# Turning q of two more batches by DMA, with a new written order, in a fused attention and channel-mix kernel

## The chip, the cores and the metric

The kernel runs on one core of a Trainium2 chip. The metric is the device time of one execution in microseconds (us); three timed executions and one profiled execution of the kernel before are known.

## The reference

There are 8 batches, 8 heads, 576 positions and 64 elements to a head. Attention here is linear: `q` is softmaxed over the head's elements, `k` over the positions, and the two are joined by a 64 x 64 matrix for each head. The result is the input of a channel mix over 512 channels with a hidden size of 1024.

```python
q_s = softmax(q, axis=-1); k_s = softmax(k, axis=2)
kv  = einsum('bhsd,bhse->bhde', k_s, v)
x   = einsum('bhsd,bhde->bhse', q_s, kv)          # heads side by side: (8, 576, 512)
x_prev = x moved down by one position, a zero row first
xk = mu_k * x + (1 - mu_k) * x_prev;  xr = mu_r * x + (1 - mu_r) * x_prev
k  = maximum(xk @ w_k, 0)                         # 512 -> 1024
out = sigmoid(xr @ w_r) * ((k * k) @ w_v)         # 1024 -> 512
```

## The kernel before

**Attention.** A batch `b` is worked in two groups `g` of four heads. A load brings q, k or v of a group in float32 into one of 11 `raw` buffers (L212, issued on GpSimd's queue for batches 1 to 7). For each group: ScalarE takes the exponentials of q and k (`expq`, `expk`, L345) and casts v (`cast`, L352); VectorE sums the exponentials of q over the head (`rsum`, L360), takes the reciprocal (`rrec`, L364) and scales (`scale`, L369), which gives q in `qs`, positions on the partitions. The next product needs q with the head's elements on the partitions, so q has to be turned. There are three ways in the code:

- Batches 0 and 1 (`FUSED`): TensorE turns q by products with an identity (`T` steps, L386), ScalarE and VectorE copy the result from PSUM (`qt`, L395). Here mu is folded into the 64 x 64 matrix, so that `X` steps (L520) give xk and xr at once and the `x` steps copy them out (L530 to L535). In names such as X1001 the digits are batch, group, which of xk (0) and xr (1), and half of the positions.
- Batches 2 to 4: the turning products stand inside the block of the group that is named `TKV` or `B` (L386), ScalarE copies q out (`qt`, L397).
- Batches 5 to 7 (`CROSS`): SyncE issues one DMA that turns all of `qs` into `qt` (`tq`, L559). It waits for `scale` and has no work on TensorE or ScalarE.

```python
        crossed = b in CROSS
            def block():
                if turn_x: turn_x[0](qtp)        # x of the group before
                if not crossed: transpose_q(qtp)
                kv(qtp)
        if crossed:
            qcopy = add("SP", lambda: kn.nc.sync.dma_start_transpose(
                out=turned_sb(), in_=kn.qss[qs.index][:].rearrange("p j c -> p (j c)")),
                scaled, [qt], [qs], name=f"tq{tag}")
        else:
            qcopy = add("ACT", lambda: copy_qt(qtp), [tr, wdone], [qt], [qtp], name=f"qt{tag}")
```

A block of batch 2 or later does three things on TensorE: x of the group before (L576), the turn of its own q (where it is not crossed), and kv (L419). `rz` and `w` (L426, L436) make the 64 x 64 matrix of a group from kv. `xb` and `xs` (ScalarE, L581 and L584) copy x out, and VectorE mixes it with the row before: `edge` (L589), `diff` (L593), four `sc` (L598), two `mix` (L603). `mix` with third digit 0 gives xk, with 1 xr.

**Channel mix.** It runs over two rings of 2304 columns (four batches). `k<unit>_<n>` steps are products of xk with one 128-wide piece of w_k over the 256 to 512 columns of a unit (L680), `relu` is on ScalarE (L659), `sq` on VectorE (L669). Tiles of 128 rows follow: `r` (xr with w_r, L713), `th` (tanh on ScalarE, L718), `v<tile>_<part>` (k squared with w_v, L733), `o` (VectorE, L739) and two stores on SyncE's queue (`st`, L749). A `.2` after a k step of units 0 to 2 is the half of its product that needs group 1.

**Order.** Nothing is scheduled at run time beyond semaphores: `ORDER` is one long written list of steps. Each engine and each DMA queue takes its own steps in the order in which they stand in it; the number behind a colon is the buffer, an engine ahead of `!` puts the step on that engine. So a step that waits holds up all that stands behind it on the same engine. (`!` has effect on loads, `cast`, `wp` and `x` steps; `qt` and `rest` have their engine written in their own code.)

**Filling.** The `fill` and `fillgap` steps (L302, L311) are products of zeros of 512 and 256 columns, of which no one reads the result. They stand in the first 15 us of TensorE's list.

Of the kernel before, what the change touches and what calls it, by code (L numbers as in the profile page):

```python
# [67 lines left out]
v3_1 DVE!qt100:1 expk101 qt101 X1101:1 KV10 edge10 ACT!x1101 edge11 rz10:0 v0_2 kvn10:1 v3_2
POOL!wp100:1 o0 v1_2 load21v0:4 X1001:1 expq200:0 o1 X1000:0 X1110:3 load21k0:5 x1001 st1 v2_0:0
x1000 load30k0:7 DVE!x1110 cast200:2 X1111:1 load31q0:6 rsum200:1 X1100:0 k2_1:2 load40q0:8 x1100  # L70
v2_1 k2_7:3 expq210:2 wp101 rrec200 o3 k2_1.2 v2_2 load61v0:9 relu2_1:0 k2_2:1 o2 k2_7.2 expq300:1
load50k0:10 k2_0:2 x1111 k2_2.2 relu2_7:1 sq2_1 k2_5:0 rsum300:0 load31k0:0 k2_0.2 expk200:1
k2_4:3 X1010:0 relu2_2:2 X1011:1 scale200:1 load40v0:1 k2_4.2 relu2_0:0 k2_3:1 x1010 k2_6:2 sq2_7
cast210:0 k2_3.2 sq2_0 load30v0:2 k2_5.2 x1011 k2_6.2 relu2_5:1 rsum210:2 TKV20:0 relu2_4:0
load40k0:3 expk210:2 r5:0 rz20:1 rrec300 rrec210 r7:3 w20:0 th5:4 sq2_5 load31v0:4 scale210:2
relu2_3:1 r6:0 qt20:0 r4:1 load41q0:5 scale300:0 th7:5 B21:1.0 expq310:0 sq2_2 sq2_4 r8:3 rz21:2
relu2_6:2 sq2_3 load41v0:6 rsum310:3 xs20:0 th4:6 v4_0:2 xb20 v6_0:1 sq2_6 w21:1 th6:7 rrec310
edge20 v4_1 diff20:0 qt21:2 v6_1 scale310:1 th8:8 X21:0.1 v5_0:0 xb21:1 sc2001:0 sc2000 v4_2 o6
xs21 expk300:0 v7_0:3 edge21 st6 mix200 v5_1 st0 cast300:1 diff21:1 load51q0:7 st3 v7_1 sc2101:1
st2.2 expk400:1 sc2100 load60q0:2 mix210 st0.2 TKV30:0 cast310:2 o7 st3.2 load41k0:3 k3_4:1 st2 o5  # L80
expq400:2 k3_0:3 load70v0:4 sc2011:2 rz30:0 sc2111:0 k3_6:0 w30:2 relu3_4:0 sc2110 load70q0:8
sc2010 relu3_0:1 o4 k3_1:1 expk310:2 mix201 k3_5:3 mix211 relu3_1:2 load61q0:0 k3_3:2 qt30:1 sq3_1
sq3_4 k3_2:1 sq3_0 relu3_3:2 rsum400:1 relu3_5:0 B31:1.0 relu3_2:1 rrec400 k3_7:2 sq3_3 xb30:0
sq3_2 sq3_5 v8_0:3 xs30 relu3_6:2 rz31:1 scale400:2 r9:1 relu3_7:1 expq410:1 v10_0:0 sq3_7 w31:0
# [6 lines left out]
load50v0:1 sq4_6 k5_5 relu4_0:1 mix311 k5_2:1 relu5_4:0 k5_7 sq4_0 cast410:2 k4_2:3 sq5_4 w40:1
scale510:1 k4_5:2 relu4_2:1 load71k0:6 relu5_6:0 k4_1:3 mix301 expq600:2 sq4_3 k5_3 sq4_2 k4_4:0
relu4_1:2 sq5_6 load60k0:2 rsum500:3 relu4_5:1 k5_0:3 relu4_4:0 r14:2 qt40:2 rsum600:1 k5_1 r13:0
th14:7 sq4_1 cast500:0 rrec600 B41:1.0 rrec500 sq4_5 sq4_4 th13:4 load60v0:1 scale600:2 v13_0:2
xs40:1 relu5_0:2 r15:0 xb40 rz41:0 sq5_0 w41:2 v12_0:3 relu5_2:1 edge40 diff40:1 th15:8 v15_0:1
qt41:1 scale500:0 v13_1 expk510:1 sc4001:0 tq50:0 B50:0.1 o13 st10.2 cast600:2 v12_1 rsum700:2
v15_1 xb41:0 rz50:1 o12 r16:0 expk610:2 w50:0 st12 sq5_2 v14_0:2 sc4010:1 st13.2 sc4000 xs41 o15
expk710:0 st13 v16_0:3 edge41 st12.2 mix400 th16:9 r17:1 st7.2 sc4011 expq710:2 diff41:0 tq51:2
B51:1.0 sc4110:2 cast610:0 v16_1 rrec700 sc4101:0 sc4100 v17_0:0 mix410 expk600:1 rz51:2 o16 v14_1
th17:1 mix401 expq610:1 k6_4:3 o14 k6_0:1 v17_1 sc4111 xs50:1 st14 xb50 w51:1 mix411 st4.2 k6_1  # L100
k6_2:2 rsum610:0 st1.2 relu6_0:0 B60:1.0 st11.2 k6_3 tq60:1 xb51:0 sq6_0 k6_5 st15.2 rz60:0
rrec610 edge50 r19:1 o17 st11 relu6_4:2 diff50:1 xs51 st16 k6_6:0 th19:4 r18:3 edge51 diff51:0
expk700:1 k6_7 sc5101:0 r20:1 sc5000:1 th18:3 sc5100 relu6_2:1 sq6_4 r21:3 w60:2 relu6_6:0 sq6_2
sq6_6 v19_0:2 th21:5 sc5010:2 mix510 th20:6 v18_0:0 sc5001 mix500 v19_1 sc5011 B61:0.1 o19 k7_3:3
sc5110:0 mix501 k7_2:1 scale700:0 relu7_3:2 xb60:1 k7_0:2 scale610:1 relu7_2:1 k7_6:3 relu7_0:0
k7_1:1 sc5111 tq61:0 rz61:1 sq7_3 tq70:2 mix511 v18_1 relu7_6:2 st14.2 cast700:1 sq7_6 k7_4:2
sq7_2 rsum710:1 relu7_1:2 k7_5:3 relu7_4:1 r23:1 o18 sq7_1 k7_7:2 sq7_0 th23:0 w61:0 relu7_5:2
r25:0 xs60 relu7_7:0 edge60 sq7_4 B70:1.0 sq7_7 rrec710 v21_0:1 diff60:1 xs61:0 xb61 v22_0:3
sc6000:1 th25:2 edge61 diff61:0 v20_0:2 cast710:2 sc6001 r22:0 rz70:2 sc6110:2 sq7_5 w70:1 v21_1
mix600 th22:7 sc6100:0 B71:0.1 sc6101 mix610 v22_1 o21 k8_1:0 scale710:2 k8_3:1 relu8_1:1 o22  # L110
tq71:1 v20_1 st19 sc6111 mix611 k8_0:0 st22 st15 sc6011:1 v23_0:3 rz71:0 relu8_0:0 st19.2 xb70:0
sq8_0 k8_4:0 st16.2 st18.2 xs70 v23_1 relu8_3:2 relu8_4:0 sq8_3 k8_5:1 sq8_4 edge70 k8_2:0 w71:2
relu8_5:2 diff70:0 sc6010 X71:1.0 o20 k8_6:1 mix601 st20.2 k8_7:2 relu8_6:0 st18 sq8_5 sq8_1 r26:1
st20 sc7010:0 relu8_7:2 sc7001:2 st17 relu8_2:1 sc7000 r28:2 xs71:1 sq8_2 xb71 o23 r24:0 th28:8
# [784 lines left out]
```

## Time and profile before

| | us |
|---|---|
| three runs | 198.82, 198.87, 199.62 (median 198.87) |
| the profiled execution | 198.85 |
| its span, first to last instruction | 196.9 |
| busy in the span: TensorE, VectorE, ScalarE | 188.0, 151.9, 134.9 |

A row of the profile's timeline gives start, duration, engine, line of the kernel, operation, what it writes and reads, shapes and count; a bracket at its end tells how long the engine had been idle and what released it. PE is TensorE, DVE VectorE, ACT ScalarE, POOL GpSimd, SP SyncE. In the views of windows a row is a stretch of the span with the busy time of each engine, the clock that TensorE was granted (PEclk, 1.00 is full), the mean busy share of the 16 DMA engines and what they moved.

### The profile page before, as it was taken

The page shows a single profiled execution, that of the slowest core. Times are in us where ns is not written, and L with a number is a line of the kernel's source. Part 1 is how long each engine was busy: PE and PEld are TensorE (multiplying, and loading weights), DVE is VectorE, ACT ScalarE, POOL GpSimd, SP SyncE. Part 2 cuts the span into 40 slices and gives each one's busy share as a digit, 9 for nine tenths or more (in the row PEclk, how much of TensorE's full clock was granted, in tenths as well). Part 3 has the DMA queues.
Part 4 walks back from the last instruction along what each step waited for, and adds up shares of the span by engine and source line. Part 5 has one row for each costly group of instructions (what it writes and reads, how often), then busy time and mean ns, then how long its engine had stood idle before and what let it go on. Part 6 is the DMA issues. An engine that isn't in the chain of part 4 may idle for free.

```text
span 196.9 us, 4779 instructions
## 1 busy us (share of the span) xinstructions
PE 188.0 (95%) x1894; PEld 96.1 (49%) x1916; DVE 151.9 (77%) x343; ACT 134.9 (69%) x213; POOL 47.7 (24%) x79
## 2 busy tenths in 40 slices
PE   7799989899999999999999999999999999999992
PEld 2268654445454455455544564444444444444441
DVE  1957599789999999999999998989868553534421
ACT  3755759879999999989999984676166345433311
POOL 5849576098312503333200000000000000000000
PEclk9966999999999999999999999999999999999998
DMA  6999999979999998989878582060274011065835
GB/s 188 348 203 295 348 256 359 398 239 392 392 389 387 315 416 297 298 312 413 318 148 168 103 171 64 16 134 0 57 168 107 0 42 41 19 142 118 202 83 160
DMA packets 23702, 41.87 MB, mean 213 GB/s; under 512 B 9460, under 2 KB 12800, under 8 KB 23680
## 3 DMA queue, kind: packets, MB, share of 16 engines
q0 software_dynamic: 9504, 28.00, 44.0%
q1 hardware_dynamic: 13360, 12.13, 25.3%
...
## 4 chain that ended last, share of the span: by engine, by line
PE 79%; DVE 9%; ACT 5%; DMA 2%; issue 2%; POOL 0%; DVEq 0%; POOLq 0%
PE mm_b L680 9%; PE mm_c L680 8%; PE mm_d L680 8%; PE mm_d L733 7%; PE mm_c L733 7%; PE mm_a L733 7%; PE mm_a L680 6%; PE mm_a L713 4%; PE mm_b L733 4%; PE mm_b L713 4%; PE mm_c L713 2%; DMA raw_a<-in_q_dram 2%; PE mm_d L713 2%; PE att_a L419 2%; PE att_b L419 1%
## 5 line engine op out<-in xcount | busy, mean ns | idle before, releaser
L733 PEld LDWEIGHTS <-k 128*128 128x128 bf16 x296 | 28.0, 98 | 31.4 <-issue 0.5
L713 PEld LDWEIGHTS <-xr 128*128 128x128 bf16 x144 | 13.8, 98 | 15.8 <-issue 0.8
L669 DVE TENSOR_TENSOR k<-rel_b 128x512 bf16<-128x512 bf16 (+2 forms) x24 | 10.2, 427 | 6.5 <-ACT rel_b L659 6.4
L669 DVE TENSOR_TENSOR k<-rel_a 128x512 bf16<-128x512 bf16 (+2 forms) x27 | 11.1, 412 | 4.2 <-ACT rel_a L659 4.0
L669 DVE TENSOR_TENSOR k<-rel_c 128x512 bf16<-128x512 bf16 (+2 forms) x25 | 10.1, 402 | 4.3 <-ACT rel_c L659 4.1
L713 PE MATMUL mm_a<-wr,xr 128*128 128x512 bf16 x47 | 12.3, 379 | 0.6 <-ACT rel_a L659 0.5
L713 PE MATMUL mm_b<-wr,xr 128*128 128x512 bf16 x46 | 12.2, 379 | 0.2
L680 PEld LDWEIGHTS <-wk_ba 128*128 128x128 bf16 x88 | 8.3, 98 | 7.8 <-issue 0.5
L680 PEld LDWEIGHTS <-wk_ab 128*128 128x128 bf16 x88 | 8.5, 98 | 7.1 <-issue 0.2
L680 PEld LDWEIGHTS <-wk_bb 128*128 128x128 bf16 x88 | 8.5, 98 | 7.1 <-issue 0.2
L680 PEld LDWEIGHTS <-wk_aa 128*128 128x128 bf16 x88 | 8.3, 98 | 7.5 <-issue 0.5
L733 PE MATMUL mm_d<-wv_a,k 128*128 128x512 bf16 (+1 forms) x43 | 10.8, 369 | 0.1
L733 PE MATMUL mm_a<-wv_a,k 128*128 128x512 bf16 (+1 forms) x39 | 9.8, 369 | 0.1
L733 PE MATMUL mm_c<-wv_a,k 128*128 128x512 bf16 x35 | 9.2, 379 | 0.1
L659 ACT ACTIVATE rel_c<-mm_d 128x512 bf16<-128x512 f32 (+1 forms) x9 | 5.2, 580 | 5.1 <-issue 3.2
L680 PE MATMUL mm_b<-xk,wk_ab 128*128 128x512 bf16 (+3 forms) x34 | 8.6, 334 | 0.0
L680 PE MATMUL mm_b<-xk,wk_aa 128*128 128x512 bf16 (+3 forms) x34 | 8.6, 334 | 0.0
L659 ACT ACTIVATE rel_c<-mm_b 128x512 bf16<-128x512 f32 (+1 forms) x8 | 4.8, 595 | 4.8 <-PE mm_b L680 4.0
L680 PE MATMUL mm_d<-xk,wk_bb 128*128 128x256 bf16 (+3 forms) x30 | 7.4, 328 | 0.0
L680 PE MATMUL mm_d<-xk,wk_ba 128*128 128x256 bf16 (+3 forms) x30 | 7.4, 328 | 0.0
L733 PE MATMUL mm_b<-wv_a,k 128*128 128x512 bf16 x27 | 7.0, 379 | 0.2 <-issue 0.2
L680 PE MATMUL mm_c<-xk,wk_bb 128*128 128x512 bf16 (+3 forms) x24 | 6.5, 352 | 0.1
(361 smaller groups left out, 507.1 us busy)
## 6 DMA issues: line engine op xcount, KB each, us to landing
...
```

The costliest lines, as they stand in the source:

```text
L419: kn.nc.tensor.matmul(kn.half(slot, r)[two[u], KVO:KVO + n], lhsT=kn.eks[ek.index][two[r], j, u, :], rhs=by, start=(j == 0), stop=(j == J ...
L659: kn.nc.scalar.activation(out=kn.rels[rel.index][:, 0:width], in_=kn.bank(kf)[:, 0:width], func=ACT.Relu, scale=HALF_ROOT)
L669: kn.nc.vector.tensor_tensor(out=to, in0=src, in1=src, op=ALU.mult)
L680: kn.nc.tensor.matmul(kn.bank(kf)[:, lo:lo + n], lhsT=kn.wk[fc // 4][ct % 2][:, ct // 2, (fc % 4) * 128: (fc % 4) * 128 + 128], rhs=kn.xs[ ...
L713: kn.nc.tensor.matmul(kn.bank(rps), lhsT=kn.xs[1][:, ct, c:c + 128], rhs=kn.wr[:, ct, :], start=(ct == 0), stop=(ct == CT - 1))
L733: kn.nc.tensor.matmul(kn.bank(vps)[:, 0:width], lhsT=kn.k2[:, ft, at:at + 128], rhs=wv_of(ft)[:, part], start=(ft == 0), stop=(ft == FT - 1))
```

## The change

`CROSS` takes in batches 3 and 4: their four groups have no turning products and no `qt` copy any more, and four `tq` DMAs more stand on SyncE's queue. Five of the fourteen `fillgap` steps go; the nine that stay are the early ones. The whole of `ORDER` is written anew (all steps but these are the same).

```diff
-GAPS = 14
+GAPS = 9
-CROSS = (5, 6, 7)
+CROSS = (3, 4, 5, 6, 7)
```

The two lists, where the last gaps and the steps of batch 0 stand:

```diff
-fillgap.4:2 fillgap.5:3 fillgap.6:2 fillgap.7:3 fillgap.8:2 expk010:1 load11q1:4 scale001:1 T01:1
-load10q0:5 expk011 fillgap.9:2 fillgap.10:3 fillgap.11:2 rz00:0 widecopy mucopy scale000 KV001
-ACT!qt011:0 KV000 rest T00 qt010 fillgap.12:2 fillgap.13:3 kvn00:0 DVE!qt000:1 Z01 POOL!wp000:0
-fillgap.14:2 qt001 KV011 wp001 KV010 load11q0 X0001:3 edge00 rz01:1 X0010:2 wr kvn01:1 x0001a
-X0000:0 edge01 wp010:1 ACT!x0001b load11k0:6 x0000a DVE!x0010 X0100:1 ACT!x0000b X0101:3 x0100a
-X0011:0 ACT!x0101b load11v1:7 x0100b k0_0:0 x0101a k1_0:1 x0011 k0_0.2 POOL!wp011 k1_0.2 k1_3:2
...
+fillgap.5:3 fillgap.6:2 fillgap.7:3 fillgap.8:2 scale010 expk010:1 load11q0:4 scale000:1
+load10q1:5 expk011 T01:1 fillgap.9:2 widecopy rz00:0 scale001 KV001 load11q1 KV000 qt011:0
+POOL!rest DVE!qt010 T00 Z01 edge01 kvn00:0 KV011 qt001:1 POOL!wp000:0 DVE!qt000 KV010 wp001
+load10q0 X0001:3 edge00 rz01:1 wr kvn01:1 X0010:0 ACT!x0001b wp010:1 X0000:1 x0001a mucopy wp011
+x0010 X0101:2 load11k0:6 DVE!x0000a X0100:3 x0000b x0101a X0011:0 x0101b DVE!x0100a load11v0:7
+X0110:1 x0100b k0_4:0 k1_7:1 DVE!x0110 k0_0:2 k1_0:3 load10v0:8 k1_7.2 x0011 k1_0.2 relu1_7:0
```

Where q of batch 1 is turned (`T10` stands behind five v steps before, ahead of them after), and where unit 4 of the channel mix begins:

```diff
-kvn11:0 load20v0:0 v0_0:3 sq0_6 th2:3 DVE!wp111:0 ACT!cast100:1 load21q0:1 v1_0:0 qt111:2 rrec100
-qt110 scale101:0 v3_0:1 load30q0:2 scale100 v1_1 wp110 cast101 v0_1 load20k0:3 expk100:0 T10:0
...
-sc3101 expq510:2 rrec410 st7 v11_1 sc3010 mix310 st4 expk410:2 r12:0 load61k0:7 scale410:0 st8
-k4_6:2 th12:3 load70k0:3 o11 expq500:1 k5_6:0 o9 k4_7:3 rsum510:0 relu4_6:0 st9.2 load51k0:5
...
+wv2 th3:0 scale100 th1:1 T11:0 load20q0:10 KV11 th2:2 T10:1 load21q0:0 qt111:2 v0_0:1 sq1_6
...
+expk410:1 mix310 v11_0:3 o8 expq510:0 k4_0:2 load51k0:7 rrec410 sc3010 v9_1 scale410:0 cast510:2
+load71q0:9 v11_1 relu4_0:1 w40:1 load60k0:0 tq41:1 o9 k5_4:0 expq600:2 o11 k4_5:2 st7 sq4_0
```

More of the change, by code (lines that the diff above doesn't have):

```diff
@@ L67 @@
-qt110 scale101:0 v3_0:1 load30q0:2 scale100 v1_1 wp110 cast101 v0_1 load20k0:3 expk100:0 T10:0
[L68 to L84, printed above, removed]
@@ L91 @@
[L91 to L108, printed above, removed]
@@ L109 @@
[L109 to L114, printed above, removed]
@@ L121 @@
-o28 sq10_4 v29_1 relu10_3:2 v31_1 sq10_3 o29 k10_5:1 sq10_2 st29 r31:0 st29.2 st24.2 k10_6:3
-th31:3 st27.2 o31 v30_0:0 relu10_6:2 relu10_5:0 st31.2 k10_1:2 st28 sq10_5 v30_1 st28.2 relu10_1:0
-st22.2 sq10_1 r34:3 sq10_6 sq10_7 st31 v32_0:1 o30 th34:5 st17.2 r32:2 st30 st23 v32_1 th32:4
-v35_0:3 o32 v33_0:0 st32.2 v34_0:2 st30.2 st32 r33:1 v33_1 th33:9 v34_1 o33 r35:1 st33.2 o34 st33
-v35_1 th35:2 st34 v35_0.2:0 st34.2 o35 v35_1.2 st35.2 st35 o35.2 st35.4 st35.3
+ACT!load01k1:3 SP!load01k0 warm POOL!muload expq000:0 expq001 load00v^expq000 rsum000:0 load01v
@@ new lines @@
+x0010 X0101:2 load11k0:6 DVE!x0000a X0100:3 x0000b x0101a X0011:0 x0101b DVE!x0100a load11v0:7
+X0110:1 x0100b k0_4:0 k1_7:1 DVE!x0110 k0_0:2 k1_0:3 load10v0:8 k1_7.2 x0011 k1_0.2 relu1_7:0
+k0_4.2 load11k1 k0_0.2 relu1_0:1 sq1_7 k0_5 k0_1 load11v1 relu0_4:2 k1_3:1 k1_4:3 expq110:2 k1_3.2
+sq0_4 wv0 k1_4.2 relu1_3:0 k1_2:0 rsum110:2 relu1_4:2 load10k1:9 X0111:1 expq100:1 k1_5:1 sq1_4
+k0_6:3 sq1_3 k1_5.2 relu0_0:2 rrec110 sq1_0 k1_2.2 rsum100:3 k0_6.2 relu1_5:0 k1_1:2 expq101
+k0_2:1 scale110:2 k1_1.2 expq111 k0_2.2 load10v1 k0_7 rsum101 k0_3 relu0_6:1 wv1 rrec100 ACT!x0111
@@ new lines @@
+rrec101 r0:3 sq1_5 sq0_0 relu1_2:0 rsum111 relu0_2:2 k1_6:0 ACT!cast110:0 sq1_2 k1_6.2 rrec111
+r3:1 sq0_2 relu1_6:0 scale111 expk111:2 r1:0 cast111 relu1_1:2 load10k0 expk110 scale101:0 r2:2
+wv2 th3:0 scale100 th1:1 T11:0 load20q0:10 KV11 th2:2 T10:1 load21q0:0 qt111:2 v0_0:1 sq1_6
+load20v0:1 rz11:2 sq0_6 expk101:0 v1_0:0 sq1_1 ACT!cast100:1 kvn11:0 cast101 wp110:0 v3_0:2 qt110
+load30q0:2 DVE!qt100:1 DVE!wp111 ACT!qt101 load20k0:3 edge11 X1101:0 v0_1 x1101 expk100 v3_1 th0:3
+KV10 X1100:0 rz10:0 edge10 v3_2 kvn10:1 x1100 POOL!wp100:1 v0_2 o3 v1_1 load21v0:5 o0 expq200:0
@@ new lines @@
+X1001:1 X1111:0 X1000:3 wp101 x1111 v2_0:1 ACT!x1001 load21k0:4 rsum200:1 x1000 v1_2 load31q0:7
+expq210:2 v2_1 o1 X1011:0 load31v0:6 k2_7:2 ACT!x1011 rrec200 load40q0:8 k2_1:3 rsum210:0
+cast200:2 k2_5:0 load30k0:9 k2_1.2 k2_7.2 relu2_1:0 load30v0:10 rrec210 k2_5.2 scale200:1
+relu2_7:1 X1010:1 X1110:0 relu2_5:2 load31k0:0 v2_2 expq300:1 sq2_5 k2_0:3 o2 k2_3:2 expk200:1
+k2_4:0 load40v0:1 DVE!x1110 st2.2 k2_3.2 DVE!x1010 st2 k2_2:1 relu2_3:2 TKV20:0 st3.2 sq2_7
+load50k0:2 expk210:2 rsum300:2 st3 k2_0.2 k2_4.2 st1.2 relu2_0:1 k2_2.2 sq2_3 cast210:0 st1 k2_6:2
@@ new lines @@
+load40k0:3 rz20:1 r6:3 w20:0 rrec300 sq2_0 relu2_4:2 scale210:2 k2_6.2 qt20:0 r4:0 scale300:0
+relu2_2:1 B21:1.0 th4:4 load41q0:4 th6:5 r7:1 sq2_1 tq30:1 rz21:2 expq310:0 sq2_4 w21:1 r5:0 sq2_2
+xs20:0 rsum310:3 load41v0:5 relu2_6:0 v6_0:3 xb20 v4_0:2 sq2_6 qt21:2 load41k0:7 rrec310 edge20
+v6_1 diff20:0 th5:6 scale310:1 X21:0.1 th7:7 v4_1 xs21:1 v5_0:0 xb21 o6 tq31:0 v7_0:1 sc2000:0
+expk300:0 edge21 sc2001 diff21:1 st6.2 r8:3 cast300:1 load51q0:9 st6 sc2011:1 v5_1 mix200 th8:8
+sc2111:2 load61q0:10 v4_2 sc2100:0 expq400:2 sc2101 TKV30:1 mix210 v7_1 cast310:2 load60q0:8 o5
@@ new lines @@
+k3_3:3 st5 o7 expk310:1 load50q0:6 o4 k3_0:0 relu3_3:2 rz30:0 load51v0:0 sc2010 k3_1:1 sc2110
+cast400:0 w30:2 mix201 k3_2:2 relu3_0:1 load61v0:1 relu3_1:0 sq3_0 B31:0.1 mix211 k3_6:3 xb30:0
+rsum400:1 k3_7:0 relu3_6:1 expk400:2 rz31:1 rrec400 r10:1 sq3_6 sq3_1 k3_5:3 scale400:2 relu3_2:1
+load61k0:3 xs30 th10:9 r9:2 w31:0 relu3_7:0 tq40:2 edge30 sq3_2 r11:1 sq3_3 relu3_5:1 diff30:0
+expq410:1 k3_4:0 st0.2 sq3_5 sq3_7 B40:1.0 relu3_4:2 sc3011:0 load50v0:4 sc3000:1 v10_0:3 sc3001
+xb31:1 sq3_4 rsum410:0 v8_0:0 xs31 th9:2 v10_1 th11:0 rz40:2 edge31 mix300 cast410:1 r12:2 o10
@@ new lines @@
+o13 st4 B51:0.1 st8 o17 st9 k6_0:3 rsum700:0 xb50:0 k6_2:1 k6_1 xs50 expk600:0 k6_4:0 rz51:2 w51:1
+k6_3 sc4111 edge50 v16_1 mix411 relu6_2:2 relu6_0:1 B60:1.0 o16 k6_5 sq6_2 xs51:1 st16.2 xb51
+r19:1 rz60:0 diff50:0 st17.2 w60:2 expk710:1 r20:3 st8.2 sc5000:2 sc5011:1 st17 edge51 sc5010
+B61:0.1 th20:0 diff51:1 relu6_4:0 k6_6:2 rsum610:1 r18:3 th19:4 cast700:2 v14_0:0 sq6_0 sc5001
+th18:2 mix501 k6_7 v14_1 sc5101:0 relu6_6:2 sc5100 v18_0:1 mix510 rrec610 r21:3 sq6_4 sc5110:1
+rz61:1 mix500 v19_0:2 th21:8 o14 k7_0:3 sc5111 st14.2 sq6_6 k7_3:0 scale610:0 relu7_0:1 v19_1
@@ new lines @@
+relu7_3:0 sq7_0 tq61:0 xb60:0 k7_6:3 o19 mix511 v18_1 st16 relu7_6:2 xs60 st19 k7_2:0 cast710:0
+o18 st13 w61:0 k7_7:2 sq7_6 expk700:0 rsum710:3 k7_1:3 k7_5:1 rrec710 relu7_1:1 rrec700 sq7_3
+relu7_2:2 r23:3 edge60 sq7_1 scale700:1 k7_4:0 th23:9 relu7_7:0 sq7_2 B70:1.0 tq70:1 diff60:0
+relu7_4:1 v20_0:3 relu7_5:2 scale710:2 xb61:1 v21_0:2 rz70:2 sq7_4 tq71:2 r22:0 xs61 sq7_7 edge61
+sq7_5 v22_0:1 th22:7 sc6001:0 st15.2 w70:1 sc6010:2 v20_1 sc6000 sc6011 mix600 v23_0:0 o20 v21_1
+diff61:1 st20.2 v22_1 st13.2 sc6100:1 sc6101 st18 B71:0.1 o22 st19.2 r25:3 mix610 rz71:0 o21 v23_1
@@ new lines @@
+mix601 st21 k8_7:1 o23 k8_0:2 w71:2 relu8_7:1 st23 sc6111:0 xs70:0 st21.2 k8_2:0 xb70 st23.2
+k8_5:1 th25:3 edge70 st20 sq8_7 relu8_0:0 sc6110 st18.2 k8_6:3 mix611 relu8_2:2 st15 k8_1:2 sq8_0
+relu8_6:1 st14 diff70:0 X71:0.1 relu8_1:0 sq8_2 r27:0 sq8_6 relu8_5:2 sc7000:1 xs71:1 k8_3:3 sq8_5
+k8_4:2 relu8_3:1 xb71 r30:1 relu8_4:2 r28:3 edge71 sq8_1 th30:4 diff71:1 r24:2 th27:8 sc7100:2
+th28:9 sq8_3 r29:1 sc7101 th24:0 mix710 v27_0:0 th29:2 sc7001 mix700 v25_0:3 sc7011:0 k10_0:2
+sq8_4 sc7110:2 sc7010 k9_6:1 v25_1 relu9_6:0 relu10_0:1 sq9_6 k9_0:1 o25 v27_1 st25 relu9_0:2
@@ new lines @@
+st25.2 r26:2 st12 k9_2:3 th26:6 v24_0:1 relu9_2:0 sq9_2 v26_0:2 sq9_0 k9_1:3 v26_1 relu9_1:0
+k9_4:3 o26 sc7111 v24_1 st26 relu9_4:2 mix711 k9_7:2 o27 o24 k9_3:3 sq10_0 k9_5:0 sq9_1 relu9_3:1
+sq9_3 k10_4:1 sq9_4 v28_0:3 relu10_4:0 relu9_5:1 v30_0:1 relu9_7:2 sq9_5 sq10_4 v29_0:0 sq9_7
+mix701 v30_1 v28_1 o30 v31_0:2 st30 o28 st24 v29_1 st28 r31:1 st27.2 st12.2 k10_5:3 th31:5 st26.2
+v31_1 st22.2 relu10_5:1 st22 sq10_5 k10_6:1 k10_2:3 relu10_6:0 sq10_6 r32:1 relu10_2:2 o31 k10_3:3
+sq10_2 st31.2 o29 st24.2 k10_1:2 relu10_3:1 st29.2 r34:0 st28.2 relu10_1:0 th32:3 st29 sq10_1
@@ L126 @@
+k10_7:3 sq10_3 th34:1 st30.2 v32_0:2 st31 relu10_7:2 st27 sq10_7 v35_0:1 v32_1 v34_0:0 o32 v33_0:3
+st32 st32.2 r33:2 v33_1 th33:6 v34_1 o33 r35:2 st33.2 o34 st33 v35_1 th35:7 st34 v35_0.2:3 st34.2
+o35 v35_1.2 st35.2 st35 o35.2 st35.4 st35.3
 """
```

32 lines of the change are left out of this document (12 added, 20 removed).

## The prediction

> **What bounds the kernel now.** I read the page first: busy time, the slices, then the chain that ended last.
>
> ```profile
> span 196.9 us, 4779 instructions
> PE 188.0 (95%) x1894; PEld 96.1 (49%) x1916; DVE 151.9 (77%) x343; ACT 134.9 (69%) x213; POOL 47.7 (24%) x79
> ...
> PE   7799989899999999999999999999999999999992
> ...
> DVE  1957599789999999999999998989868553534421
> ...
> PEclk9966999999999999999999999999999999999998
> ...
> PE 79%; DVE 9%; ACT 5%; DMA 2%; issue 2%; POOL 0%; DVEq 0%; POOLq 0%
> ```
>
> TensorE is busy for 95% of the span and 79% of the last chain is its own. VectorE stands at 9 in nearly every slice up to two thirds of the span, so it is the one to come next. The shares are averages; the stages show in the view of windows (stretch, its length, then busy time and count for TensorE, weight loads, VectorE, ScalarE, GpSimd; then granted clock, DMA share, GB/s):
>
> ```profile
> 12.00:18.00 6.00, 6.00 (x155) 4.79 (x159) 3.35 (x13) 2.70 (x7) 4.04 (x9) 0.50 1.20 257
> 18.00:22.00 4.00, 4.00 (x42) 2.58 (x39) 1.55 (x3) 2.02 (x6) 2.91 (x6) 0.98 1.17 278
> 28.00:40.00 12.00, 10.88 (x159) 4.93 (x159) 10.07 (x27) 9.18 (x16) 5.24 (x10) 1.00 1.07 361
> 42.00:64.00 22.00, 21.84 (x274) 10.60 (x268) 20.99 (x39) 21.32 (x31) 10.07 (x16) 1.00 1.00 382
> 64.00:134.00 70.00, 69.05 (x817) 36.29 (x820) 66.80 (x143) 61.81 (x91) 10.96 (x16) 1.00 0.74 223
> ```
>
> From 12 to 18 TensorE is full, but at half its clock. From 12 to 22 VectorE is idle for 2.65 + 2.45 = 5.1 us. From 28 to 40 TensorE has 1.12 us of holes. From 42 to 134 it is full (0.16 + 0.95 us of holes) and VectorE has 1.01 + 3.20 us left. So a product that goes from TensorE's list pays in full after 42, as long as VectorE can follow.
>
> The sum is made on the profiled execution, 198.85 us, of which 1.95 lie around the span of 196.9; the median of the three runs is 198.87, the same within 0.02.
>
> **The turning products.** Two blocks, one of batch 3 with 18 products and one of batch 4 with 36; the first row of each pair is the turn, the second the kv that follows:
>
> ```profile
> 63.70 0.43 PE L386 MATMUL att_a<-ident,qs_a 64*128 64x64 bf16 x18
> 64.06 0.48 PE L419 MATMUL att_a<-vv_b,ek_a 64*64 64x65 bf16 x36
> ...
> 96.42 0.48 PE L386 MATMUL att_b<-ident,qs_a 64*64 64x64 bf16 x36
> 96.72 0.49 PE L419 MATMUL att_b<-vv_c,ek_c 64*64 64x65 bf16 x36
> ```
>
> From start to start the turn takes 0.36 us in the whole form (group 0 of batch 3) and 0.30 in the other (three groups): 0.36 + 3 x 0.30 = 1.26 us leave a stretch in which TensorE is full. The four copies of q on ScalarE go too; ScalarE holds TensorE up nowhere in this stretch for long (all holes there are 0.95 us), so I count them at 0, between 0 and 0.95 gained. What comes is four turning DMAs on SyncE's queue:
>
> ```profile
> 74.37 0.86 PE mm_a L733 x4
> ...
> 127.00:132.00 5.00, 5.00 (x25) 2.27 (x24) 4.25 (x9) 3.83 (x8) 0.00 (x0) 1.00 0.75 144
> ...
> DMA to landing us min/median/max: 3.2/3.3/4.6
> ...
> 96.01 1.15 ACT L352 CAST vv_a<-raw_b 128x1152 bf16<-128x1152 f32 x1 [0.24 <-DMA raw_b<-in_v_dram]
> ```
>
> The second row holds two of them and one store: 5.00 x 0.75 = 3.75 us of all 16 DMA engines, so one takes at most 1.9 and four at most 7.5. The third row is the time from issue to landing of the six that are there now. Priced by the first row (0.86 us for four products of 512 columns), at least 12 us of TensorE's steps stand in the new list between each of the four and the block that reads it, so a landing two and a half times as long costs nothing. Behind them on SyncE stand stores only, for which nobody waits as long as one of the ten `th` buffers is free. In the last row ScalarE waits 0.24 us for a load. In the new list the loads that follow the first new `tq` stand at least 15 us of such steps ahead of their readers, so I count their lateness at 0 (bound at the rival). GpSimd's queue loses `wp011`, and its loads stand behind one product less.
>
> **The five gaps.**
>
> ```profile
> 11.32 0.42 PE L311 MATMUL mm_d<-rel_c 128*128 128x256 bf16 x1
> ...
> 11.88 0.99 PE L419 MATMUL att_a<-xd_a,ek_a 64*64 64x64 bf16 x36
> ...
> 13.40 0.40 PE L311 MATMUL mm_c<-rel_c 128*128 128x256 bf16 x1
> ...
> 13.94 0.40 PE L406 MATMUL att_b<-one,ek_b 64*128 64x1 bf16 x18
> 14.27 0.39 PE L311 MATMUL mm_c<-rel_c 128*128 128x256 bf16 x1
> 14.60 0.88 PE L419 MATMUL att_b<-xd_b,ek_b 64*64 64x64 bf16 x32
> 15.25 0.44 PE L520 MATMUL mm_c<-qt_b,wp_a 64*64 64x288 bf16 x1
> ...
> 14.51 0.46 DVE L395 COPY qt_b<-att_a 128x576 bf16<-128x576 bf16 x1 [0.70 <-ACT qt_b L395]
> ```
>
> Two stand from 11.32 to 11.88, two from 13.40 to 13.94, one from 14.27 to 14.60: 0.56 + 0.54 + 0.33 = 1.43 us. But the X step at 15.25 also needs the copy of q that VectorE ends at 14.97, and only the first 0.56 us stand ahead of that. So X can start at 14.4 at the earliest, 0.85 us sooner; if the clock comes back at 18 as before, that is 0.85 us of work at half clock, worth 0.42 at full clock. I take 0.35, between 0 (the start is held by something else) and 1.43 (all of it pays).
>
> **The new order.** Its risk is that TensorE reaches a step sooner than VectorE has made its input. The tightest such place that I find is the first product of unit 4, which needs `mix310`:
>
> ```profile
> 82.45 0.75 DVE L603 TENSOR_TENSOR xk<-xm_a,xb_b 128x1152 bf16<-128x1152 bf16 x1
> ...
> 83.93 0.59 PE L680 MATMUL mm_c<-xk,wk_ba 128*128 128x512 bf16 x2
> ...
> 18.12 0.46 DVE L530 CAST xk<-att_b 128x288 bf16<-128x288 f32 x1 [0.47 <-ACT xk L530]
> 18.50 0.75 DVE L532 CAST xr<-att_a 128x576 bf16<-128x576 f32 x1
> 21.15 0.43 DVE L669 TENSOR_TENSOR k<-rel_b 128x512 bf16<-128x512 bf16 x1 [1.91 <-ACT rel_b L659]
> 22.47 0.75 DVE L532 CAST xr<-att_b 128x576 bf16<-128x576 f32 x1
> ...
> 24.62 0.70 DVE L532 CAST xr<-att_a 128x576 bf16<-128x576 f32 x1
> ...
> 16.16 0.76 DVE L509 TENSOR_TENSOR wp_b<-kvn_b,mu_wide 128x128 bf16<-128x128 f32 x2
> ...
> 84.39 0.68 DVE L739 SCALAR_TENSOR_TENSOR th_c<-th_c,mm_d 128x512 f32<-128x512 f32 x1
> ```
>
> *TensorE:* ahead of unit 4 the new list lacks `v9_1` and `v11_1` (0.86 each, the row at 74.37), three of the four turns (0.96) and the gaps (0.35), and nothing is added. It would be there at 83.93 - 1.72 - 0.96 - 0.35 = 80.9. *VectorE:* in the old list it ended `mix310` at 83.20. In the new one it does the copies of batch 0 early: from `wp010`, at 16.16 - 0.35 = 15.8, two wp (0.76 each; one was GpSimd's), five half copies (0.46 each; four were ScalarE's) and the two copies of 18.50 and 22.47 (0.75 each) come to 5.3 us, so its first `sq` starts at 21.1 in place of 21.15, with the copy of 22.47 done already and that of 24.62 given to ScalarE. Of the later steps `o8` (0.68) now stands behind `mix310`; the other copies that change engines cancel. That is 0.05 + 0.75 + 0.70 + 0.68 = 2.2 us, and `mix310` ends at 81.0: VectorE is there 0.1 us behind TensorE, if it loses nothing new by the way. The other moved step is `T10`, which waited for VectorE before:
>
> ```profile
> 34.64 1.36 DVE L369 TENSOR_TENSOR qs_a<-eq_b,rrec_d 128x576 bf16<-128x576 bf16 x2
> ...
> 36.06 0.44 PE L386 MATMUL att_a<-ident,qs_a 64*128 64x64 bf16 x18 [0.15 <-DVE qs_a L369]
> ```
>
> Five v parts that stood ahead of it stand behind it now (three of 0.86, two of 0.43), so TensorE comes at 36.06 - 3.44 - 0.35 = 32.3. VectorE's scale ended at 36.00; with 1.5 us of lead by then it would be 34.5, a wait of 2.2, but a kvn, a wp, an rz, a copy of q and three sq that stood ahead of this scale stand behind it now and take most of that off. A wait here is not paid again at unit 4. For both places together I take 0.3 us, between 0 and 2.2. For the holes from 28 to 40, of which a VectorE that is ahead can close some, I take 0.3 of the 1.12 gained, between 0 and 1.12.
>
> **Sum:** 198.85 - 1.26 - 0.35 - 0.3 + 0.3 = 197.24, so 197.2 us. Its own range is 196.2 to 197.8.
>
> **The rivals.**
>
> *VectorE falls behind (slower).* The five half copies stand one behind another on VectorE, each behind its X product at half clock; if the first `sq` comes at 23.3 and not at 21.1, the 2.2 us of lead are gone. TensorE then waits 2.3 at unit 4, and at the start up to two half copies (0.92) for its first k steps: 198.85 - 1.61 + 2.3 + 0.92 = 200.5. It decides from a first `sq` at about 22.9 on, where in proportion the time passes 199.85. For it: VectorE has 4.2 us left in 92 us. Against it: 5.1 idle us stand just where the copies go. With half of the lead lost the time is about 198.8.
>
> *The clock stays low.* It is 0.50 from 12 to 18 and back at 0.98 from 18 on, and the gap at 11.32 took 0.42 us already, so the low stage is about 6.7 us. It ends after about 3 us of X products without any fill; its first half held the gaps and did not bring the clock back. If the thinner list delays the return by half of the stage again, 3.4 us at half clock cost 1.7: 197.2 + 1.7 = 198.9. Against it: the products that stand ahead of the return stay. [...]
>
> *The DMA becomes late.* Share 1.00 from 42 to 64; 7.5 us of transposing would push the loads back by as much. If a quarter of that reaches TensorE, 1.9: 199.1. [...]
>
> *All of the ramp pays.* 198.85 - 1.26 - 1.43 - 1.12 = 195.0.
>
> That the products do not go is no rival: the built list of TensorE is shorter by 252 rows of turning and 10 of filling.
>
> **Chances.** A measurement of this kernel tells 0.5% (1.0 us) from no change, so faster is below 197.87 and slower above 199.85. The forecast has 0.48 and the good ramp 0.09: faster 0.57. Half of the lead lost 0.09, the clock 0.07, the DMA 0.07: the same 0.23. VectorE behind: slower 0.20. The range 195.9 to 200.1 leaves out the best ramps and the worse half of the slow rival.
>
> **What would show it.** Right: no L386 rows after 60; holes of TensorE from 42 to 134 no more than 1.4 us; the first `sq` (L669) at 20.5 to 22; the first product of unit 4 at 80.5 to 81.5 with VectorE's `xk` (L603) just ahead; the clock back at 18; the new DMAs landed over 5 us ahead of their blocks. Wrong: TensorE's rows of L680 with idle time that a DVE row of L603 ended, the clock at 0.5 after 19, or ScalarE's casts waiting for loads by more than 1 us.

## The result, and the profile after

The changed kernel takes 211.96 us (median of four runs, 211.66 to 212.88) against 199.14 (198.82 to 199.62): 1.065 times the time before, 95% interval 1.0606 to 1.0693. The forecast was 197.2, with a range up to 200.1. The profiled execution took 212.23 us. Here and below the ratios leave out executions that were disturbed, so a median beside a ratio can lie a little off.

From the page of the changed kernel, the lines that answer to those of before:

```profile
span 210.5 us, 4561 instructions
PE 190.6 (91%) x1785; PEld 94.7 (45%) x1785; DVE 151.5 (72%) x345; ACT 131.3 (62%) x209; POOL 46.5 (22%) x76
...
PE   7987999999994399999549999999999999999990
...
PEclk9999999999999589999957999999999999999998
...
q0 software_dynamic: 9504, 28.00, 43.2%
q1 hardware_dynamic: 18096, 13.31, 27.5%
...
PE 69%; DMA 20%; DVE 4%; ACT 3%; issue 1%; ACTq 0%
```

Two notches stand in TensorE's row that were not there before, each with a dip of the granted clock right behind it, and a fifth of the last chain is now a DMA. The view of windows, with the stretches of the prediction first and the two notches after them:

```profile
12.00:18.00 6.00, 4.34 (x146) 2.96 (x137) 5.14 (x20) 2.84 (x6) 3.29 (x6) 1.00 1.20 260
...
28.00:40.00 12.00, 12.00 (x189) 5.58 (x187) 9.85 (x24) 10.39 (x19) 8.81 (x15) 1.00 1.08 359
42.00:64.00 22.00, 22.00 (x283) 10.62 (x282) 21.40 (x45) 22.00 (x32) 9.78 (x14) 1.00 1.03 361
64.00:134.00 70.00, 58.29 (x566) 29.92 (x565) 52.64 (x113) 47.33 (x69) 8.87 (x13) 0.90 0.81 220
...
65.50:71.80 6.30, 0.00 (x1) 0.03 (x1) 2.08 (x3) 0.18 (x1) 0.22 (x1) 0.75 1.06 384
71.80:75.50 3.70, 3.66 (x51) 1.74 (x50) 0.33 (x2) 1.62 (x3) 0.00 (x0) 0.50 1.07 373
102.60:108.10 5.50, 0.16 (x1) 0.10 (x1) 2.66 (x6) 1.43 (x2) 0.00 (x0) 0.83 0.99 200
108.10:113.00 4.90, 4.87 (x53) 2.19 (x53) 2.65 (x4) 1.68 (x3) 0.00 (x0) 0.50 0.78 218
```

Up to 64 all is well: TensorE has no hole from 28 to 40 and from 42 to 64. Then it stands still twice, and after each hole it works at half the clock for 3.7 and 4.9 us. What it waited for is in the timeline, in TensorE's rows first, then in SyncE's and GpSimd's:

```profile
71.84 0.27 PE L576 MATMUL att_a<-qt_b,w_c 64*64 64x64 bf16 x4 [6.34 <-DMA qt_b<-qs_a]
108.13 0.27 PE L576 MATMUL att_b<-qt_b,w_c 64*64 64x64 bf16 x4 [5.37 <-DMA qt_b<-qs_a]
...
51.49 3.90 SPq L559 DMA_TRANSPOSE qt_b<-qs_a  x1
56.95 12.09 SPq L559 DMA_TRANSPOSE qt_a<-qs_b  x1
77.70 1.29 SPq L559 DMA_TRANSPOSE qt_c<-qs_c  x1
89.29 2.10 SPq L559 DMA_TRANSPOSE qt_b<-qs_a  x1
...
76.84 0.72 POOL L212 DMA_DIRECT2D raw_d<-in_k_dram  x1 [11.12 <-ACT ek_c L345]
```

and in the chain of waits, where a DMA's piece is the time from its issue to its landing:

```profile
51.49 20.31 DMA qt_b<-qs_a
89.29 18.79 DMA qt_b<-qs_a
```

The first and the fourth of the new transposes (`tq30`, `tq41`) land 20.3 and 18.8 us after their issue. The second (`tq31`) takes longest, 20.6 us, and its issue alone holds SyncE 12.1 us; TensorE does not wait for it. The third, issued at 77.70 when GpSimd had issued one load in 12 us, cost TensorE nothing.

**Where the 13.4 us of the profiled runs went** (212.23 - 198.85): holes 6.34 + 5.37 = 11.7; the half clock behind them costs half of 3.7 + 4.9, 4.3; together 16.0. Against them stand the 1.26 us of turning products, and 1.4 us that I do not assign.

**Why a transpose takes 20 us there.** Queue q1 has 4736 packets more than in the kernel before, whose page says

```profile
q1 hardware_dynamic: 13360, 12.13, 25.3%
```

Each new transpose is 1152 packets of 256 bytes (and 32 small ones), which is 72 for each of the 16 DMA engines if they are spread evenly. I counted the trace's DMA records in the stretch in which the first transpose is under way and TensorE stands still. In each us there:

```
load packets, 4608 bytes, 0.188 us each:           80
transposing packets, 256 bytes, 0.018 us each:   87 to 92
```

With the 7 to 12 records of 4 bytes that the loads' queue has in each us, that is one to one. I read it as turns: a transposing packet goes, then a packet of the loads' queue, then the next; the records do not name the engine. Over the whole of the first transpose, 55.5 to 70.7, its 1152 packets run beside 1058 load packets and 131 records of 4 bytes of the same queue. 72 turns of 0.188 + 0.018 = 0.206 us are 14.8 us, and the stretch has 15.2; the other 5 of the 20.3 us lie before the first packet (4.0) and behind the last (1.1). With no loads beside them the 1152 packets of a transpose pass in 1.5 to 1.6 us in five of the six of the kernel before (2.7 in the first), which is what lies behind the 3.2 us of landing that the prediction used.

The count does not come out for the fourth transpose. Its 1152 packets run from 93.5 to 107.2 beside 503 load packets and 63 small records only, and 62 of these load packets took over 0.4 us each and make half of the load packets' time. So its 18.8 us are as long as turns would have made them, but packets that were slow themselves have a large part in them, and why they were slow stays open (see the experiment with the old order).

### The profile page after: what moved, and what is told of

Its sections match the earlier page's. It is cut to its first block, busy times and chain, and to the rows that moved or that the text cites. A ratio compares the mean times of both kernels' runs of the same rounds, so it can differ in the third digit from the quotient of the medians.

```text
span 210.5 us, 4561 instructions
## 1 busy us (share of the span) xinstructions
PE 190.6 (91%) x1785; PEld 94.7 (45%) x1785; DVE 151.5 (72%) x345; ACT 131.3 (62%) x209; POOL 46.5 (22%) x76
## 4 chain that ended last, share of the span: by engine, by line
PE 69%; DMA 20%; DVE 4%; ACT 3%; issue 1%; ACTq 0%
DMA qt_b<-qs_a 19%; PE mm_d L680 9%; PE mm_a L733 8%; PE mm_b L733 7%; PE mm_d L733 6%; PE mm_c L733 6%; PE mm_c L680 5%; PE mm_a L680 5%; PE mm_b L680 4%; PE mm_c L713 4%; PE mm_d L713 3%; PE mm_b L713 3%; DMA raw_a<-in_q_dram 2%; PE mm_a L713 2%; PE att_a L520 1%
## 5 line engine op out<-in xcount | busy, mean ns | idle before, releaser
L659 ACT ACTIVATE rel_b<-mm_d 128x512 bf16<-128x512 f32 (+2 forms) x16 | 9.4, 585 | 8.7 <-PE mm_d L680 6.6
L733 PE MATMUL mm_a<-wv_a,k 128*128 128x512 bf16 x40 | 11.2, 404 | 0.0
L713 PE MATMUL mm_d<-wr,xr 128*128 128x512 bf16 x40 | 10.5, 384 | 0.2 <-ACT rel_b L659 0.2
L659 ACT ACTIVATE rel_a<-mm_b 128x512 bf16<-128x512 f32 (+1 forms) x9 | 4.9, 545 | 8.9 <-PE mm_b L680 8.8
L581 ACT CAST xb_a<-att_b 128x1024 bf16<-128x1024 f32 x5 | 5.1, 1014 | 7.9 <-issue 6.9
L733 PE MATMUL mm_b<-wv_a,k 128*128 128x512 bf16 (+1 forms) x40 | 9.9, 369 | 0.0
L680 PE MATMUL mm_d<-xk,wk_aa 128*128 128x512 bf16 (+3 forms) x36 | 9.6, 348 | 0.0
L680 PE MATMUL mm_d<-xk,wk_ab 128*128 128x512 bf16 (+3 forms) x36 | 9.6, 348 | 0.0
L713 PE MATMUL mm_c<-wr,xr 128*128 128x512 bf16 x32 | 9.1, 410 | 0.0
L713 PE MATMUL mm_a<-wr,xr 128*128 128x512 bf16 x28 | 7.2, 379 | 0.0
```

The source lines that it names most:

```text
L581: kn.nc.scalar.copy(out=kn.xbs[xb.index][:, :, 64:576], in_=kn.whole(pair))
L659: kn.nc.scalar.activation(out=kn.rels[rel.index][:, 0:width], in_=kn.bank(kf)[:, 0:width], func=ACT.Relu, scale=HALF_ROOT)
L680: kn.nc.tensor.matmul(kn.bank(kf)[:, lo:lo + n], lhsT=kn.wk[fc // 4][ct % 2][:, ct // 2, (fc % 4) * 128: (fc % 4) * 128 + 128], rhs=kn.xs[ ...
L713: kn.nc.tensor.matmul(kn.bank(rps), lhsT=kn.xs[1][:, ct, c:c + 128], rhs=kn.wr[:, ct, :], start=(ct == 0), stop=(ct == CT - 1))
L733: kn.nc.tensor.matmul(kn.bank(vps)[:, 0:width], lhsT=kn.k2[:, ft, at:at + 128], rhs=wv_of(ft)[:, part], start=(ft == 0), stop=(ft == FT - 1))
```

## The experiments

Theory A says that the transposes are late because they meet the loads on the DMA engines. All ratios are to the kernel before on the same chip.

**The turning back on TensorE, all else as changed.**

```
-CROSS = (3, 4, 5, 6, 7)
+CROSS = (5, 6, 7)
-tq30:1 ... tq31:0 ... tq40:2 ... tq41:1
+w30:2 qt30:1 ... w31:0 qt31:0 ... w40:1 qt40:2 ... w41:2 qt41:1
```

> The changed kernel with batches 3 and 4 turned by TensorE again (252 products and four copies on ScalarE back, no transposing DMA before batch 5; everything else, the new order and the nine gap fills, kept). Theory A, the crossbar transposes are late because they share the DMA engines with the loads: both holes (6.3 and 5.4 us) and the half clock behind them go, TensorE ends near 191, the time is 196.5 to 198. Rival B, the new order itself starves TensorE and the late transposes are only where it shows: the time stays over 203.

Measured: 198.80 us, ratio 1.0000 (0.9989 to 1.0011). Theory B falls: the new order alone costs nothing. The whole loss hangs on the four transposes. But the time is 0.8 over theory A's range: the new order and the nine gaps by themselves are worth nothing. The windows of this kernel and its timeline show why:

```profile
12.00:18.00 6.00, 5.66 (x138) 4.81 (x134) 5.07 (x18) 2.59 (x6) 3.27 (x6) 0.50 1.20 263
...
64.00:134.00 70.00, 67.43 (x763) 35.07 (x772) 64.01 (x136) 60.83 (x88) 8.95 (x13) 1.00 0.66 208
```

```profile
73.09 0.59 PE L680 MATMUL mm_a<-xk,wk_ba 128*128 128x512 bf16 x2 [0.58 <-ACT rel_a L659]
87.25 0.59 PE L680 MATMUL mm_b<-xk,wk_ba 128*128 128x512 bf16 x2 [0.38 <-ACT rel_a L659]
93.44 0.38 PE L680 MATMUL mm_c<-xk,wk_aa 128*128 128x256 bf16 x2 [0.62 <-ACT rel_b L659]
```

From 64 to 134 TensorE has 2.57 us of holes, where before it had 0.95. In these three rows, 1.58 us together, k products wait for ScalarE's `relu` steps. The ramp's gain (unit 2 begins at 40.60 here and at 40.48 in the changed kernel, at 42.30 in the kernel before) is given back at least in part there.

**The crossing alone, in the old order.**

```
-CROSS = (5, 6, 7)
+CROSS = (3, 4, 5, 6, 7)
+scale300:0 tq30:1 ... scale310:1 tq31:0 ... scale400:2 tq40:2 ... scale410:0 tq41:1
-qt30:1 ... qt31:0 ... qt40:2 ... qt41:1
```

> The kernel before, its order and its 14 gap fills kept, with only q of batches 3 and 4 turned by the crossbar; each transpose stands right behind the scale that makes its input, or behind the step that frees its target. Theory A: transposes issued at about 55, 60 and 85 land 15 to 20 us later, a transpose that meets no loads in 3 to 5; the leads here are 16, 18 and 17 us, so TensorE waits 1 to 9 us in all, and the time is 199 to 209, likeliest 203. Rival B: 197.5 to 198 (1.26 us of turning products less, no wait).

Measured: 224.43 us, ratio 1.1142 (1.1084 to 1.12): the wait is there without the new order, as A says, but far dearer than I had it. TensorE's two waits for transposes in the timeline, and a window between them:

```profile
75.19 0.27 PE L576 MATMUL att_b<-qt_b,w_c 64*64 64x64 bf16 x4 [4.61 <-DMA qt_b<-qs_a]
87.36 0.27 PE L576 MATMUL att_a<-qt_a,w_a 64*64 64x64 bf16 x4 [3.00 <-DMA qt_a<-qs_b]
```

```profile
66.00:74.00 8.00, 4.35 (x20) 1.79 (x19) 6.27 (x14) 4.52 (x8) 1.84 (x3) 0.95 1.35 60
```

The waits are of the size that was expected (7.6 of 1 to 9 us), but the time is far over its range of 199 to 209. From 66 to 74 the DMA engines count as busy (1.35) and move 60 GB/s, where loads and stores moved 382 from 42 to 64 before. In the DMA records of that stretch a transposing packet takes 0.19 us (median of 620), ten times its 0.018, and of the 70 load packets 16 take over 0.4 us, the longest 3.3. The stores are late too (ScalarE waits 9.3 us for one), and TensorE waits 3.17 us for that step of ScalarE. Why packets are slow in such stretches I can't say.

**Loads held while a transpose is under way.** `loadX^tqY` makes GpSimd issue the load only after the transpose has landed.

```
-load41k0:7   load51q0:9   load60v0:8
+load41k0^tq30:7   load51q0^tq31:9   load60v0^tq41:8
```

> The changed kernel, with three loads that GpSimd issues next after a transpose made to wait until that transpose has landed (k of batch 4 group 1 behind the first, q of batch 5 group 1 behind the second, v of batch 6 group 0 behind the fourth). Theory A: the loads already in flight (about six of 1.5 us) run out after 9 us, so the first transpose lands 10 to 11 us after its issue in place of 20.3, the fourth about 9 in place of 18.8; both are there before TensorE wants them (14 and 13 us), and the time is 195.5 to 198.5. Rival C, a transpose at this place takes about 20 us of itself (its issue, its source, its target), whatever else runs: landings stay at 19 to 20, and the time at 212 or over.

Measured: 202.45 us, ratio 1.0179 (1.0158 to 1.02), 9.5 us better than the changed kernel, but not the 195.5 to 198.5 of theory A. The first transpose lands in 15.57 us, where 20.31 had been measured and 10 to 11 expected. So C falls: the same transpose at the same place is quicker with fewer loads beside it (in `held_more_b` below all land in 11.2 us or less). But the lateness moved; the waits in TensorE's timeline:

```profile
67.22 0.22 PE L576 MATMUL att_a<-qt_b,w_c 64*64 64x64 bf16 x4 [1.60 <-DMA qt_b<-qs_a]
90.95 0.22 PE L576 MATMUL att_a<-qt_c,w_b 64*64 64x64 bf16 x4 [3.53 <-DMA qt_c<-qs_c]
```

The first is 1.6 us late in place of 6.3, the fourth is in time, and the third, beside which only 11 load packets had run before, now meets the burst of held loads and is 3.5 late. It lands in 19.1 us, and its 1152 packets run beside 1091 load packets and 142 small records: one to one again.

**Smaller load packets.** Each load of batches 2 to 7 as two DMAs (`raws[i][:, 0, :]`, then `raws[i][:, 1, :]`).

> The changed kernel, with each load of batches 2 to 7 issued as two DMAs of half the columns, so that a packet of a load has 2304 bytes and not 4608. Theory A in its sharp form, each of the 72 packets that a transpose has for one DMA engine waits for one packet of a load: with packets half as long (about 0.10 us in place of 0.19) the first transpose lands in 10 to 12 us and the fourth in 9 to 11; holes under 1 us, time 196 to 201. Theory A in a loose form, a transpose waits until the queued loads are through: the same bytes are queued, landings stay at 18 to 20, and the time at 210 or over.

Measured: 226.21 us (222.54 to 230.84), ratio 1.1195 (1.1167 to 1.1223). It tells nothing on the packet's size: the DMA records still have 5376 load packets of 4608 bytes, and 576 more small ones. So this kernel does not test the sharp form, and why the time rose is open.

**A transpose cut over two queues**, which gave the cleaner test of the turns.

```
+kn.nc.scalar.dma_start_transpose(out=turned_sb()[:, 5:9], in_=src[:, 640:1152])
+kn.nc.sync.dma_start_transpose(out=turned_sb()[:, 0:5], in_=src[:, 0:640])
```

> The changed kernel with each transpose of batches 3 and 4 cut in two DMAs, five blocks of 128 columns from SyncE's queue and four from ScalarE's. Theory A in its sharp form, a DMA engine takes one packet from each queue in turn: a queue then has 40 or 32 packets for an engine and not 72, so the first transpose lands about 13 to 15 us after its issue in place of 20 and the fourth about 10 to 12 in place of 19; TensorE's holes shrink to 0 to 2 us each, while ScalarE pays some 1.3 to 3 us for each of its four issues; 200 to 206 in all. Loose form, a transpose waits for whatever load bytes are queued: landings stay at 18 to 20 and the time at 212 or over.

Measured: 219.86 us, ratio 1.1053 (1.1016 to 1.1091). From its chain of waits, and from the timeline of ScalarE:

```profile
51.52 13.57 DMA qt_b<-qs_a
```

```profile
65.17 1.29 ACTq L563 DMA_TRANSPOSE qt_b<-qs_a  x1
66.51 1.16 ACT L345 ACTIVATE eq_a<-raw_h 128x1152 bf16<-128x1152 f32 x1 [14.75 <-issue]
```

SyncE's part, 640 packets, lands in 13.57 us where 1152 took 20.31, at the same moment of the kernel. So 512 packets, 32 for each engine, cost 6.74 us, 0.211 us each: the 0.206 of one load packet and one transposing packet. In the records the 640 packets run beside 547 load packets and 75 small ones. The loads do not have to run out; the first transpose agrees with the sharp form of A. The time is over the expected 200 to 206. The two parts did not run side by side: ScalarE's was issued at 65.17, 0.08 us after SyncE's had landed at 65.09, ScalarE did nothing else for 14.75 us, and TensorE then waited for ScalarE and not for a transpose:

```profile
68.32 1.87 PE L738 MATMUL mm_c<-wv_a,k 128*128 128x512 bf16 x4 [14.14 <-ACT rel_a L664]
```

Why ScalarE's part was not issued sooner no run shows.

**Half of the change at a time.** `CROSS = (3, 5, 6, 7)`, and `CROSS = (4, 5, 6, 7)`, the other batch's tokens put back as in the first experiment.

> The changed kernel with batch 4 turned by TensorE again, batch 3 still by the crossbar. If each late transpose costs by itself: the first hole (6.3 us, and 1.75 us for the half clock behind it) stays, the second goes; 198.8 - 0.66 + 8.05 = 206.2, between 204 and 207.5. If the holes only come as a pair: 198 to 200.

> The changed kernel with batch 3 turned by TensorE again, batch 4 still by the crossbar. If each late transpose costs by itself: the two transposes follow each other in the queue while loads run, the second is 5 to 7 us late at its block, and the half clock behind it costs 2; 205 to 208. If the second hole was a child of the first (loads that GpSimd could not issue during the first hole came bunched into the time of the fourth transpose): both land in time, 198 to 199.5.

Measured: 206.05 us (1.036, 1.0314 to 1.0407) and 203.90 us (1.025, 1.0215 to 1.0285). Their waits, first with batch 3 alone, then with batch 4:

```profile
71.80 0.27 PE L576 MATMUL att_a<-qt_b,w_c 64*64 64x64 bf16 x4 [6.31 <-DMA qt_b<-qs_a]
```

```profile
99.70 0.27 PE L576 MATMUL att_b<-qt_b,w_c 64*64 64x64 bf16 x4 [3.55 <-DMA qt_b<-qs_a]
```

Each pair costs by itself: 7.3 and 5.1 us over the kernel with none, 12.4 of the 13.2 together. The first came out as the sum had it (206.2); the second is under its range of 205 to 208. The second hole is 3.55 without the first in place of 5.37: part of it was its child, most was not.

**More holds.** Four holds, and the six stores that stood ahead of `tq30` moved behind `tq31`; the three kernels differ in the loads that are held.

```
load41v0^tq30  load51q0^tq31  load50q0^tq40  load60v0^tq41      (held_more)
load41v0^tq30  load51q0^tq31  load61k0^tq40  load60v0^tq41      (held_more_b)
load41q0^tq30  load51q0^tq31  load61v0^tq40  load60v0^tq41      (held_mid)
```

> The changed kernel with four loads held (v of batch 4 group 1 until the first transpose has landed, q of batch 5 group 1 until the second, q of batch 5 group 0 until the third, v of batch 6 group 0 until the fourth) and six stores of SyncE's queue moved behind the second transpose, where they stood ahead of the first. Theory A: every transpose meets at most four or five loads in flight and no stores, lands within 12 us and before TensorE asks; what is left is the gain of the change itself, 1.3 us of turning products and some waits on ScalarE's four copies: 196.5 to 198.3, the first version under both kernels. Rival D, what is taken from the transposes comes back as loads that are late for ScalarE: no transposes in TensorE's waits, but ScalarE's exp or cast steps wait over 2 us for loads, and the time is 199 to 202.

> The same, but the third hold stands three loads later (k of batch 6 group 1). Theory A: six loads are in flight when the third transpose is issued, three more than in the sister kernel, so it lands some 5 us later, 12 to 15 us after its issue; TensorE waits for it 0 to 1 us; time 196.8 to 199. Rival D: the later hold costs ScalarE less, so this kernel is the faster of the two by about 1 us.

> Between the two kernels with held loads: q of batch 4 group 1 held until the first transpose has landed (one load earlier than before), q of batch 5 group 1 until the second, v of batch 6 group 1 until the third, v of batch 6 group 0 until the fourth; the six stores behind the second transpose. In the better of the two the first transpose landed only 2.7 us before its block and the third 4.4, its runs lie between 197.7 and 201.3. Theory A: with 1.5 us more of lead for both, the scatter goes and the time is 197.5 to 198.5, under both kernels. Rival D: the loads held are now what is late, ScalarE waits over 2 us for one, 199 to 202.

Measured: 202.23 us (1.0165, 1.0139 to 1.0191); 200.18 (1.0008, 0.9972 to 1.0043; single runs from 197.67 to 201.27); 201.37 (1.0112, 1.0079 to 1.0144). In all three profiles TensorE waits for no transpose any more. In the first and the third the loads are late in their place, rival D. The rows are ScalarE's wait for a load and TensorE's wait for ScalarE, for `held_more`, then for `held_mid`:

```profile
84.98 1.15 ACT L352 CAST vv_c<-raw_a 128x1152 bf16<-128x1152 f32 x1 [5.43 <-DMA raw_a<-in_v_dram]
86.68 1.01 PE L680 MATMUL mm_c<-xk,wk_ba 128*128 128x512 bf16 x2 [4.65 <-ACT rel_b L659]
```

```profile
89.92 1.16 ACT L345 ACTIVATE ek_c<-raw_d 128x1152 bf16<-128x1152 f32 x1 [3.61 <-DMA raw_d<-in_k_dram]
91.79 1.02 PE L713 MATMUL mm_b<-wr,xr 128*128 128x512 bf16 x4 [2.86 <-ACT rel_a L659]
```

`held_more_b` has the same waits, smaller, in its profiled execution (197.99 us): ScalarE waits 2.55 us for a load at 88.18, and TensorE 1.78 us for ScalarE. Its row, the landings of its transposes, and its window:

```profile
90.05 1.02 PE L713 MATMUL mm_b<-wr,xr 128*128 128x512 bf16 x4 [1.78 <-ACT rel_a L659]
```

```profile
DMA to landing us min/median/max: 3.2/4.5/11.2
```

```profile
64.00:134.00 70.00, 67.54 (x660) 34.56 (x670) 65.36 (x141) 56.98 (x85) 12.28 (x18) 1.00 0.82 245
```

So with every transpose in time this one execution is some 0.8 us under the kernel before (median 198.77). Four of the ten runs lie at 197.67 to 198.64, six at 199.92 to 201.27, and the ratio shows no gain: that the crossing is worth anything here is not shown. No version beats the kernel before.

**The gap fills alone.** `GAPS = 9` and `fillgap.10` to `.14` out of the kernel before.

> The kernel before with nothing changed but the five late gap fills taken out (14 to 9). My second step said 0.35 us gained (between 0 and 1.43): 198.5. Theory E, the stretch up to 30 us is bound by VectorE, ScalarE and the loads and not by TensorE, whatever clock it has: no change, within 0.15 us of the kernel before. Rival, fewer fills bring the low clock more often or for longer: 199.2 or over.

Measured: 198.51 us, ratio 0.9989 (0.997 to 1.0009): the interval holds both no change and my 0.35. Its window shows what matters more:

```profile
12.00:18.00 6.00, 4.47 (x118) 2.82 (x111) 4.15 (x14) 3.17 (x9) 4.70 (x9) 1.00 1.20 263
```

## Why the prediction was wrong

**The step that failed is the landing of the new transposes**, in the part on the turning products. I took 3.2 to 4.6 us from the six that were there, allowed two and a half times that, and set 12 us of TensorE's steps against it. The steps were there (14.0 and 13.5 us), but the transposes landed in up to 20.6 us, and TensorE stood still for 6.34 and 5.37. The rows were from the wrong stretch. The old six run after 100, with no load packet beside them (0 records of 4608 bytes while their packets run). The new ones were issued at 51, 57 and 89, where the DMA engines are full: the share of 1.00 from 42 to 64 I had quoted, and around 89 it is no lower. From the kernel before, an old transpose and that stretch:

```profile
101.42 1.40 SPq L559 DMA_TRANSPOSE qt_a<-qs_a  x1
...
88.00:90.00 2.00, 1.95 (x16) 1.47 (x15) 1.91 (x6) 1.97 (x4) 0.72 (x1) 1.00 1.04 412
```

I bounded their cost as bandwidth, 1.9 us of all engines each, and asked how far they push the loads. The direction was the other one: the loads push them, the first one by about a packet of the loads' queue for each of its own (1189 beside 1152). A warning was there: the page of before has 9460 packets under 512 bytes, of which the six transposes make 6912, and in its DMA records 80 to 87 load packets begin in each us from 51 to 63 and 45 to 67 from 86 to 93. What a small packet pays beside loads no trace of before shows.

**The rival "the DMA becomes late"** named the right resource with 0.07 and 199.1 us. Both were too small, from the same mistake. What was missing is in the changed kernel's trace and in none of before: about one packet of the loads' queue to each packet of the first transpose (1189 to 1152), and 5 us before and behind the packets. With both, my estimate of the landing is 5 + 72 x 0.21 = 20 us against leads of 13.5 to 14, some six us late where loads run as they did there. That is the first wait (6.34), from which the estimate is made. The second (5.37) has the size too, but not by turns alone, so there the agreement is in part luck.

**What a hole costs** was not in the sum at all: after 6.3 and 5.4 us of standing still the clock was 0.50 for 3.7 and 4.9 us, 4.3 us of work lost. Shorter holes go both ways in these runs: behind the 3.55 us with batch 4 alone the page's PEclk row falls to 5 tenths, and four products of 512 columns took 1.89 and 1.91 us (at 100.82 and 102.50; 1.03 at 106.44); behind the 3.53 us with held loads the row stays at 9, and four such products took 1.03 (at 93.38). How long a hole has to be for the low clock is not shown.

**The turning products, 1.26 us:** neither shown nor refuted. With four transposes in time, `held_more_b` ran at 197.99 in the profile beside 198.8, but six of its ten runs are over 199.9.

**The gaps and the ramp, -0.35 and -0.3:** X began at 14.15 (forecast 14.4), the holes from 28 to 40 went (1.12 to 0), but the time did not: the gaps are worth 0.26 with zero in the interval, and the whole order 0.0. The lead was gone by 134, at least in part in waits for `relu`.

**VectorE, +0.3:** the waits did not come. From the changed kernel:

```profile
14.15 0.28 PE L520 MATMUL mm_c<-qt_b,wp_a 64*64 64x288 bf16 x1 [0.55 <-ACT qt_b L395]
19.81 0.32 DVE L669 TENSOR_TENSOR k<-rel_a 128x320 bf16<-128x320 bf16 x1 [0.41 <-ACT rel_a L659]
30.96 0.44 PE L386 MATMUL att_b<-ident,qs_a 64*128 64x64 bf16 x18
82.86 0.75 DVE L603 TENSOR_TENSOR xk<-xm_b,xb_a 128x1152 bf16<-128x1152 bf16 x1
87.09 0.59 PE L680 MATMUL mm_c<-xk,wk_aa 128*128 128x512 bf16 x2
```

The first `sq` came at 19.81 and not 21.1, `T10` at 30.96 without a wait, and unit 4 at 87.09, which is 78.9 without the first hole and its half clock (6.34 + 1.85 us), with no wait for `xk`. The slow rival that I gave 0.20, VectorE behind, did not happen; the time rose by another road.
